# A spectral filter and a channel MLP on one core: the first group's norm written shorter, w1's sums on TensorE, and the folds' rows issued behind other blocks

## The chip, the cores and the metric

The kernel runs on one core of a Trainium2 chip. The metric is the device time of one execution in microseconds. Six actors appear below: PE (TensorE, matmuls and the weight loads before them, PEld), DVE (VectorE), ACT (ScalarE), POOL (GpSimd), SP (SyncE, which here only issues DMAs), and the 16 DMA engines. Every engine works through its own queue in order; an instruction that waits on a semaphore holds up whatever is queued behind it on that engine.

## The reference

x has 2048 rows of 448 numbers. It is normalised over the row, and two branches of the result are added to x:

```
xn = layernorm(x)
A  = irfft2(rfft2(xn) * (w_r + 1j * w_i))
h  = gelu(layernorm(xn) @ w1)                  # 448 x 448
hs = (h with its four column groups shifted by +1, -1, +2, -2 rows) @ w2
x1 = xn + hs
B  = x1 + gelu(layernorm(x1) @ w3) @ w4        # 448 x 1792, 1792 x 448
out = x + A + B
```

All inputs are fp32. The two norms in a row (the second one inside branch B) differ only by the eps terms, so the kernel gets both scales from one mean and one variance.

## The kernel before, in words

**Tiling.** The rows are split so that row a * 16 + b is partition a of block b: 16 blocks of 128 x 448. They form four groups, `GRP` = [14, 15, 0, 1], [2, 3, 4, 5], [6, 7, 8, 9], [10, 11, 12, 13], in which a shift by one or two rows is a shift to a neighbouring block. A group lies in one tile `xt`.

**Number format.** Matmuls run in fp16 on pairs: a matrix is scaled by a power of two and split into a high half and the rest, and three of the four products are summed in PSUM. For each weight matrix the scale comes from the sum of its squares: ACT squares the matrix and sums along the row (`squares`, L246), DVE adds the few columns up and PE adds over the partitions with a matrix of ones (`powers`, L251 and L258), and DVE takes the exponent out of the bits (L261 to L264) and gives the scale s and its inverse r. `split_w` then makes the halves; for the first quarter of w1 on DVE (L273, L275).

**The head.** SP issues the loads: x of group 0 in two halves, w1, x of group 1, w2, x of group 2, two of the four pieces of w3 (`w3raw`), x of group 3, the other two pieces. PE meanwhile runs `WARM` matmuls of zeros (L890). `stats1` takes mean and variance of each block on DVE (L316, L317). `norm1` makes from them a rough inverse square root, by the integer trick on the float's bits: `va` = variance plus eps terms, for the outer and the inner norm (L342, L343), shift and subtract into `vy` (L344, L345), -mean times that into `nma` (L347). Then each block is normalised in place with it, by the engine that `apply` names (L360 on DVE or POOL, L357 on ACT; in group 0 POOL takes the first 128 columns of the block that ACT has, L355). The exact root is made later, on POOL (`refine`, L368 to L376), and goes in with the scales `gsc` and `cs`. The list passed for group 0 is P, V, V, A, and `mid=squares1` puts ACT's squares of w1 between `nma` and the normalisation.

After that PE turns the blocks of group 0, one quarter of the columns at a time (`turn_pe`, L414), into `pta`; ACT and DVE make the halves (`turn_copy`, L424, L425, into `w4x`), and PE multiplies with w1 (`w1_in`, L465). Each further quarter needs its halves of w1: on POOL L281, L283, L286, L289, on ACT L282, L288. Between PE's matmuls of the first group the rows of group 1 are normalised and turned in the same way (second use of L342 to L360 and L414).

**From h to the MLP.** `w1_unit` makes gelu and halves of h (ACT L486, L488, DVE L489) into `hs` or a piece of `x2mem`, and a transposing DMA on SP turns each block of it into `h` (L492). `w2_mm` multiplies with w2 (L510), for block b from the blocks b - 1, b + 1, b - 2, b + 2. Groups 2 and 3 of x are turned by transposing DMAs too (`turn`, L911). `ln2` normalises for the MLP and turns by DMA (L553, its last block leaves the keys "b0", "b4", "b8" and so on). The MLP runs over pairs of blocks G and pairs of 128 columns of the inner 1792, fp = 0 to 6: `front` (L435, into PSUM `pw`, with gelu on ACT, L774, and halves on ACT and DVE, L777, L778) and `back` (L812, into `acc`).

**The spectral branch** is laid between the MLP's matmuls. `do_fold` loads the rows of x again, two blocks at a time, into one of four buffers (L575: three are `xf`, in the place that w2 and h leave; the fourth is `hgm`), ACT normalises them (L579, L580), POOL folds (L584 to L587), ACT and DVE make halves `xh` (L595, L596), and `step1` multiplies (L605, into `ps`).

**What sets the order.** A planner orders each engine's queue on its own model of time. `behind(key)` pins what is issued inside it behind the instructions that left that key, where they stand on the same engine; it adds an order and no wait. `PACE` pins `step1` of the blocks 0 and 1 behind the MLP's `back` of (0, 6), and so on; `FOLD` pins ACT's part of the folds behind the halves of `front`.

Of the kernel before, what the change touches and what calls it, by code (L numbers as in the profile page):

```python
# [26 lines left out]
WARM = 22  # L27
# [3 lines left out]
EPS = 1e-5  # L31
# [91 lines left out]
def body(tc, nc, x, wf, w1, w2, w3, w4, c_g, c_n, c_small, out):  # L123
# [41 lines left out]
    def xb(b):  # L165
        g, i = WHERE[b]
        return xt[g][:, i]
# [80 lines left out]
    def powers(m, n, key, tag="acc", mid=None, pin=None, down=0):  # L248
# [10 lines left out]
        after["p" + key] = (i.ins,)  # L259
        e = pc.tile([128, 3], I32, name=f"pe{key}")  # L260
# [3 lines left out]
        i = V.tensor_scalar(out=e[:, 2:3], in0=e[:, 0:1], scalar1=1, scalar2=(69 + down) << 23, op0=ALU.mult, op1=ALU.add)  # L264
        after["s" + key] = (i.ins,)
        return e.bitcast(F32)[:, 1:2], e.bitcast(F32)[:, 2:3]
# [28 lines left out]

    def rsqrt(r, a, n, key):
# [3 lines left out]
        V.tensor_single_scalar(i, a.bitcast(I32), 1, op=ALU.logical_shift_right)  # L300
        V.tensor_scalar(out=i, in0=i, scalar1=-1, scalar2=0x5F3759DF, op0=ALU.mult, op1=ALU.add)
# [29 lines left out]
    def norm1(g, apply, seen=0, mid=None):  # L331
# [8 lines left out]
        y = yi.bitcast(F32)  # L340
        with behind(0, 3) if g == 2 else contextlib.nullcontext():
            V.tensor_scalar(out=a[:, n:], in0=mv[:, :n, 1], scalar1=1.0 + EPS, scalar2=EPS * EPS, op0=ALU.mult, op1=ALU.add)  # L342
            V.tensor_scalar(out=a[:, 0:n], in0=mv[:, :n, 1], scalar1=EPS, scalar2=None, op0=ALU.add)  # L343
        V.tensor_single_scalar(yi, a.bitcast(I32), 1, op=ALU.logical_shift_right)  # L344
        V.tensor_scalar(out=yi, in0=yi, scalar1=-1, scalar2=0x5F3759DF, op0=ALU.mult, op1=ALU.add)  # L345
        nm = pc.tile([128, n], F32, name=f"nma{b0}")
        i = V.scalar_tensor_tensor(out=nm, in0=mv[:, :n, 0], scalar=-1.0, in1=y[:, n:], op0=ALU.mult, op1=ALU.mult)  # L347
        if mid:
            mid()
        for k, b in enumerate(bs):  # L350
            y_, m_ = y[:, n + k:n + k + 1], nm[:, k:k + 1]
            if apply[k] is A:
                o = 128 if g == 0 else 0
                if o:
                    P.tensor_scalar(out=xb(b)[:, :o], in0=xb(b)[:, :o], scalar1=y_, scalar2=m_, op0=ALU.mult, op1=ALU.add)  # L355
                with behind("sq", g) if ("sq", g) in after else contextlib.nullcontext():
                    i = A.activation(out=xb(b)[:, o:], in_=xb(b)[:, o:], func=AF.Identity, scale=y_, bias=m_)  # L357
# [841 lines left out]
```

## Time and profile before

| | us |
|---|---|
| median of 3 runs (408.83 to 409.05) | 408.83 |
| the profiled execution | 408.91 |
| its span, first to last instruction | 406.4 |

| engine | idle longest before | us in all, times |
|---|---|---|
| POOL | `e` L735, for ACT | 56.5, 14 |
| ACT | `pw` L774, for PE | 42.6, 34 |
| DVE | `hf` L778, for ACT | 36.8, 25 |
| PE | the first warm-up matmul L890, for DVE | 1.2, 1 |

A row of the profile reads: start in us from the span's first instruction, us, engine, source line, operation, what it writes <- what it reads, partitions x elements and type, how many instructions the row merges, and in brackets how long the engine had been idle before and what ended that. SPq is SP's queue: the duration of a DMA row there is the time of its issue, not of the transfer; the time to landing is told apart. In the rows by stretches stand, after the length, busy us and instructions of PE, PEld, DVE, ACT and POOL, then the granted clock of TensorE, the DMA engines' busy share and GB/s. The chain of work that ended last is followed back from the last instruction; its rows are start, us and what.

### The profile page before, as it was taken

The numbers are of one execution on the slowest core, as the hardware profiler recorded it, in microseconds if no ns is written. First come the engines' busy times: TensorE is split into PE (matmuls) and PEld (weight loads), VectorE is DVE, ScalarE is ACT, GpSimd is POOL, SyncE is SP. The second block draws the span as 40 slices with busy tenths as digits, with TensorE's granted clock in tenths as the row PEclk, the third lists the DMA queues.
The fourth block names the chain that finished last, engine by engine and source line by source line (L and its number), as shares of the span: only waits on it lengthen the run. The fifth ranks groups of instructions, "written<-read, shape, count | busy, mean of one in ns | idle before, by whom it ended". The sixth has DMA issues, their size and how long they took to land.

```text
span 406.4 us, 8829 instructions
## 1 busy us (share of the span) xinstructions
PE 401.0 (99%) x3379; PEld 295.9 (73%) x3379; DVE 304.0 (75%) x664; ACT 268.4 (66%) x465; POOL 173.0 (43%) x270
## 2 busy tenths in 40 slices
PE   8999999999999999999999999999999999999996
PEld 3554556666677877776878878877788888888885
DVE  5989998898554757893677777773588879889645
ACT  4699984984738766862587888776856566444332
POOL 3889803011099746599143434431232264211000
PEclk9999999999999999999999999999999999999999
DMA  8999999905910383417064566632000112233201
GB/s 283 379 245 183 175 176 253 272 2 113 242 57 0 96 276 129 115 34 177 15 147 129 144 151 163 157 93 58 2 2 2 47 45 77 86 96 112 89 2 45
DMA packets 57209, 49.46 MB, mean 122 GB/s; under 512 B 41312, under 2 KB 52192, under 8 KB 57168
## 3 DMA queue, kind: packets, MB, share of 16 engines
q1 hardware_dynamic: 57168, 48.91, 46.1%
q8 instruction: 26, 0.43, 0.5%
q14 instruction: 15, 0.12, 0.1%
HBM read 35.06 MB, written 3.67 MB: 95 GB/s over the span
## 4 chain that ended last, share of the span: by engine, by line
PE 83%; DVE 7%; DMA 3%; ACT 3%; issue 1%; POOL 0%; SPq 0%; DVEq 0%; ACTq 0%
PE pw L435 28%; PE acc L812 22%; PE pw L510 8%; PE pw L465 6%; PE pu L708 3%; PE ps L605 3%; PE pp L662 2%; PE px L679 2%; PE cr L827 2%; PE acc L827 2%; DVE xr L560 1%; DMA out<-xr 1%; PE pe L728 1%; PE py L750 1%; DVE hf L778 1%
## 5 line engine op out<-in xcount | busy, mean ns | idle before, releaser
L435 PE MATMUL pw<-x2mem,w3p 128*128 128x256 f16 x1232 | 149.2, 272 | 0.0
L435 PEld LDWEIGHTS <-w3p 128*128 128x128 f16 x1232 | 118.8, 98 | 19.4
L812 PE MATMUL acc<-w4p,hf 128*128 128x448 f16 x508 | 107.6, 352 | 0.0
L812 PEld LDWEIGHTS <-hf 128*128 128x128 f16 x532 | 51.4, 98 | 35.4
L778 DVE SCALAR_TENSOR_TENSOR hf<-pw,h,hf 128x512 f16<-128x512 f32 x56 | 41.8, 747 | 37.0 <-ACT hf L777 36.8
L774 ACT ACTIVATE pw<-pw,pe 128x512 f32<-128x512 f32 x56 | 36.7, 656 | 42.7 <-PE pw L435 42.6
L777 ACT ACTIVATE hf<-pw,h 128x512 f16<-128x512 f32 x56 | 38.3, 684 | 1.3
L510 PE MATMUL pw<-w2p,h 112*128 112x448 f16 x192 | 39.0, 352 | 0.1
L735 POOL TENSOR_TENSOR e<-e 128x226 f32<-128x226 f32 x16 | 11.0, 688 | 64.0 <-ACT e L732 56.5
L465 PE MATMUL pw<-w1p,w4x 128*128 128x448 f16 x176 | 34.8, 352 | 0.5 <-DVE h L968 0.5
L510 PEld LDWEIGHTS <-h 112*128 112x128 f16 x192 | 18.6, 98 | 16.3 <-DMA h<-x2mem 0.9
L689 POOL TENSOR_TENSOR xr<-te 128x450 f32<-128x450 f32 x16 | 15.7, 981 | 34.1 <-DVE te L687 34.1
L465 PEld LDWEIGHTS <-w4x 128*128 128x128 f16 x176 | 17.0, 98 | 16.4 <-ACT w4x L424 0.7
L697 POOL TENSOR_TENSOR zb<-xr,zb 128x450 f16<-128x450 f32 x16 | 16.2, 1011 | 17.1 <-ACT zb L696 17.1
L742 ACT ACTIVATE vh<-e 128x448 f16<-128x448 f32 x16 | 9.2, 575 | 15.6 <-DVE e L740 15.4
L685 DVE SCALAR_TENSOR_TENSOR te<-px,sc,wc 128x450 f32<-128x450 f32 x16 | 11.0, 686 | 10.3 <-ACT te L684 6.7
L684 ACT ACTIVATE te<-px 64x450 f32<-64x450 f32 x32 | 17.3, 539 | 1.7 <-PE px L679 1.2
L720 ACT ACTIVATE U<-y 113x512 f16<-113x512 f16 x32 | 18.0, 620 | 0.1
L732 ACT ACTIVATE e<-pe 128x452 f32<-128x452 f32 x16 | 8.7, 544 | 12.7 <-PE pe L728 10.2
L712 DVE SCALAR_TENSOR_TENSOR y<-pu,y 113x512 f16<-113x512 f32 x16 | 10.9, 687 | 6.9 <-ACT y L711 6.8
L540 POOL TENSOR_SCALAR y<-xt,nm 128x448 f32<-128x448 f32 x6 | 5.9, 991 | 22.8 <-DMA x2mem<-y 12.9
L584 POOL TENSOR_TENSOR xr<-xf 128x452 f32<-128x452 f32 x6 | 6.7, 1123 | 20.6 <-ACT xf L580 10.5
(207 smaller groups left out, 793.1 us busy)
## 6 DMA issues: line engine op xcount, KB each, us to landing
wc<-wf SPq DMA_DIRECT2D x32, 225.0 KB, 3.8
wl<-wf SPq DMA_DIRECT2D x8, 450.0 KB, 3.9
xt<-x SPq DMA_DIRECT2D x3, 896.0 KB, 10.2
w3raw<-w SPq DMA_DIRECT2D x3, 896.0 KB, 14.0
xf<-x SPq DMA_DIRECT2D x6, 448.0 KB, 3.9
xr<-x SPq DMA_DIRECT2D x12, 224.0 KB, 2.5
out<-xr SPq DMA_DIRECT2D x12, 224.0 KB, 2.0
gn<-c_g SPq DMA_DIRECT2D x16, 128.0 KB, 3.1
```

The lines of the kernel that those rows point to most:

```text
L435: m = T.matmul(ps_out, wp[:, wi + t, cols], xT[:, xi + t, tok], start=t == 0 and wi + xi == 0, stop=t == 3 and wi == 4)
L465: m = T.matmul(pm[:, :D], xTs[g][:, xi + t, 128 * i:128 * i + 128], w1p[:, wi + t], start=t == 0 and p == 0, stop=t == 3 and p == 2)
L510: m = T.matmul(w2b[b][:, :D], hT[g][:112, 4 * hi + k, o:o + 128], w2p[:, wi, k], start=k == 2 and hi + wi == 0, stop=k == 3 and hi == 1)
L684: i = A.activation(out=e[64 * h:64 * h + 64], in_=px_[64 - 64 * h:128 - 64 * h, :2 * DF], func=AF.Copy)
L689: P.tensor_tensor(out=z, in0=t[:, 0], in1=t[:, 1], op=ALU.add)
L697: P.tensor_tensor(out=zv[1], in0=z, in1=zv[0], op=ALU.subtract)
L720: A.activation(out=U[b][:113, p].rearrange("p q (c k) -> p q c k", c=NC), in_=Y1[:113, p, :, :, b], func=AF.Copy)
L774: A.activation(out=pm, in_=pm, func=AF.Gelu_apprx_tanh, scale=r3)
L777: i = A.activation(out=h[:, 0], in_=pv_, func=AF.Copy, scale=h3)
L778: j = V.scalar_tensor_tensor(out=h[:, 1], in0=pv_, scalar=h3, in1=h[:, 0], op0=ALU.mult, op1=ALU.subtract)
L812: m = T.matmul(to, h[:, hi, 2 * f + i], w4p[0][:, wi, 2 * fp + f, r], start=fp == s and f == 0 and hi + wi == 0, stop=fp == e and f == 1 a ...
L827: m = T.matmul(to, h[:, hi, slot] if slot < 4 else g[:, hi, slot - 4], w4f[fp][k][wi], start=k in (0, 6) and fp == 0 and hi == 0, stop=hi ...
```

## The change

- `WARM` goes from 22 to 18 matmuls.
- `guess` makes the rough root in one operation, times -0.5 and plus the constant, where a shift and a multiply-add stood (`norm1` and `rsqrt`).
- `norm1` of group 0 makes only the inner norm's row of `va` and `vy` ahead of the normalisation, and the outer one's behind it (`rough(0)`, `guess`, behind the key ("n", 0)). The other groups keep both in front.
- Group 0 is normalised by V, V, P, V for the blocks 14, 15, 0, 1; block 1 in two pieces, columns 0 to 127 and 128 to 447. ACT has no part in it, and the squares of w1 are issued ahead of `norm1`.
- `norm1` returns `y[:, n:]` in place of `nma`, so the single matmul before the last two warm-up matmuls reads that.
- The sum over w1's five columns of squares is made by PE: five matmuls with the ones into one column of PSUM, the constant column and columns 0 to 2 ahead of the first transposes, column 3 behind them. `powers` is split: `factors` gives s at once and r by a call, which is made after the high half of w1's first quarter.
- The loads of the folds' rows are pinned behind key "b4" (the transpose of block 7 in `ln2`) in place of "b8" (of block 11).

```diff
@@ -24,7 +24,7 @@
 CS = {b: 4 * g + i for b, (g, i) in WHERE.items()}
 PASS = ((0, 0), (0, 1), (1, 0))
 SHIFT = [1, -1, 2, -2]
-WARM = 22
+WARM = 18
 ZPRE = 2.0 ** -7
 UPRE = 2.0 ** -3
 VPRE = 2.0 ** -3
@@ -257,13 +257,21 @@
         with behind(*pin) if pin else contextlib.nullcontext():
             i = T.matmul(pm[:, 0:1], ones, t, start=True, stop=True)
         after["p" + key] = (i.ins,)
+        s, r = factors(pm, key, down)
+        return s, r()
+
+    def factors(pm, key, down=0):
         e = pc.tile([128, 3], I32, name=f"pe{key}")
         V.tensor_scalar(out=e[:, 0:1], in0=pm.bitcast(I32)[:, 0:1], scalar1=1, scalar2=0x7F800000,
                         op0=ALU.logical_shift_right, op1=ALU.bitwise_and)
         V.tensor_scalar(out=e[:, 1:2], in0=e[:, 0:1], scalar1=-1, scalar2=(185 - down) << 23, op0=ALU.mult, op1=ALU.add)
-        i = V.tensor_scalar(out=e[:, 2:3], in0=e[:, 0:1], scalar1=1, scalar2=(69 + down) << 23, op0=ALU.mult, op1=ALU.add)
-        after["s" + key] = (i.ins,)
-        return e.bitcast(F32)[:, 1:2], e.bitcast(F32)[:, 2:3]
+
+        def inverse():
+            i = V.tensor_scalar(out=e[:, 2:3], in0=e[:, 0:1], scalar1=1, scalar2=(69 + down) << 23, op0=ALU.mult, op1=ALU.add)
+            after["s" + key] = (i.ins,)
+            return e.bitcast(F32)[:, 2:3]
+
+        return e.bitcast(F32)[:, 1:2], inverse
 
     def absmax(out_, in_):
         V.tensor_reduce(out=out_, in_=in_, axis=AX.X, op=ALU.max, apply_absolute_value=True)
@@ -293,12 +301,14 @@
+    def guess(i, a):
+        V.tensor_scalar(out=i, in0=a.bitcast(I32), scalar1=-0.5, scalar2=0x5F3759DF, op0=ALU.mult, op1=ALU.add)
+
     def rsqrt(r, a, n, key):
...
-        V.tensor_single_scalar(i, a.bitcast(I32), 1, op=ALU.logical_shift_right)
-        V.tensor_scalar(out=i, in0=i, scalar1=-1, scalar2=0x5F3759DF, op0=ALU.mult, op1=ALU.add)
+        guess(i, a)
@@ -328,7 +338,7 @@
             mvs[g] = pc.tile([128, 4, 2], F32, name=f"mva{GRP[g][0]}")
         stats([xb(GRP[g][k]) for k in ks], f"a{GRP[g][ks[0]]}", mvs[g][:, ks[0]:])
 
-    def norm1(g, apply, seen=0, mid=None):
+    def norm1(g, apply, seen=0):
 
         bs = GRP[g]
         n, b0 = len(bs), bs[0]
@@ -338,27 +348,31 @@
         a = pc.tile([128, 2 * n], F32, name=f"va{b0}")
         yi = pc.tile([128, 2 * n], I32, name=f"vy{b0}")
         y = yi.bitcast(F32)
+        nm = pc.tile([128, n], F32, name=f"nma{b0}")
+
+        def rough(k):
+            V.tensor_scalar(out=a[:, n * k:n * k + n], in0=mv[:, :n, 1], scalar1=1.0 + EPS * k, scalar2=EPS ** (1 + k),
+                            op0=ALU.mult, op1=ALU.add)
+
         with behind(0, 3) if g == 2 else contextlib.nullcontext():
-            V.tensor_scalar(out=a[:, n:], in0=mv[:, :n, 1], scalar1=1.0 + EPS, scalar2=EPS * EPS, op0=ALU.mult, op1=ALU.add)
-            V.tensor_scalar(out=a[:, 0:n], in0=mv[:, :n, 1], scalar1=EPS, scalar2=None, op0=ALU.add)
-        V.tensor_single_scalar(yi, a.bitcast(I32), 1, op=ALU.logical_shift_right)
-        V.tensor_scalar(out=yi, in0=yi, scalar1=-1, scalar2=0x5F3759DF, op0=ALU.mult, op1=ALU.add)
-        nm = pc.tile([128, n], F32, name=f"nma{b0}")
-        i = V.scalar_tensor_tensor(out=nm, in0=mv[:, :n, 0], scalar=-1.0, in1=y[:, n:], op0=ALU.mult, op1=ALU.mult)
-        if mid:
-            mid()
+            rough(1)
+            if g:
+                rough(0)
+        guess(yi[:, 0 if g else n:], a[:, 0 if g else n:])
+        V.scalar_tensor_tensor(out=nm, in0=mv[:, :n, 0], scalar=-1.0, in1=y[:, n:], op0=ALU.mult, op1=ALU.mult)
         for k, b in enumerate(bs):
-            y_, m_ = y[:, n + k:n + k + 1], nm[:, k:k + 1]
+            x_, y_, m_ = xb(b), y[:, n + k:n + k + 1], nm[:, k:k + 1]
             if apply[k] is A:
-                o = 128 if g == 0 else 0
-                if o:
-                    P.tensor_scalar(out=xb(b)[:, :o], in0=xb(b)[:, :o], scalar1=y_, scalar2=m_, op0=ALU.mult, op1=ALU.add)
-                with behind("sq", g) if ("sq", g) in after else contextlib.nullcontext():
-                    i = A.activation(out=xb(b)[:, o:], in_=xb(b)[:, o:], func=AF.Identity, scale=y_, bias=m_)
+                i = A.activation(out=x_, in_=x_, func=AF.Identity, scale=y_, bias=m_)
                 after["na", g] = (i.ins,)
             else:
-                i = apply[k].tensor_scalar(out=xb(b), in0=xb(b), scalar1=y_, scalar2=m_, op0=ALU.mult, op1=ALU.add)
+                for c in ((slice(0, 128), slice(128, D)) if not g and k == 3 else (slice(0, D),)):
+                    i = apply[k].tensor_scalar(out=x_[:, c], in0=x_[:, c], scalar1=y_, scalar2=m_, op0=ALU.mult, op1=ALU.add)
                 after["n" if apply[k] is V else "np", g] = (i.ins,)
+        if not g:
+            with behind("n", 0):
+                rough(0)
+                guess(yi[:, 0:n], a[:, 0:n])
 
         q, z = (pc.tile([128, 2 * n], F32, tag=f"v{t}", bufs=2, name=f"v{t}{b0}") for t in "qz")
         w, r = (pc.tile([128, 2 * n], F32, name=f"v{t}{b0}") for t in "wr")
@@ -391,7 +405,7 @@
             P.tensor_scalar(out=nm1, in0=nm1, scalar1=-1.0, scalar2=None, op0=ALU.mult)
             for k, b in enumerate(bs):
                 xn_scale[b], xn_bias[b] = r1st[:, k:k + 1], nm1[:, k:k + 1]
-        return refine, gain, scales, nm
+        return refine, gain, scales, y[:, n:]
 
     after = {}
 
@@ -571,7 +585,7 @@
     def do_fold(b0):
         f = xf_buf[b0 // 2 % 4]
         X = f.rearrange("p b s d -> p (b s d)")[:, 0:2 * D + 2].rearrange("p (b d) -> p b d", b=2)
-        with behind("b8"):
+        with behind("b4"):
             after["X", b0] = (SY.dma_start(X[:, :, 0:D], xv[:, b0:b0 + 2]).ins,)
         with behind("f", *FOLD[b0 // 2]):
             for i in range(2):
@@ -934,11 +948,9 @@
         w4f[fp] = [[x[:, i] for i in range(2)] for x in (b[0][0], b[1][0], b[1][1], t4)]
         w4f[fp] += [t1] + [[x[:, i] for i in range(2)] for x in (t2, t3)]
 
-    def squares1():
-        for t in range(4):
-            n = 128 if t < 3 else 64
-            i = squares(m1[:n, t:t + 1], w1s[:n, t])
-        after["sq", 0] = (i.ins,)
+    for t in range(4):
+        n = 128 if t < 3 else 64
+        squares(m1[:n, t:t + 1], w1s[:n, t])
 
     def warm_on(src, n):
 
@@ -946,11 +958,22 @@
         with behind("on"):
             warm_up(n)
 
-    n1 = [norm1(0, [P, V, V, A], mid=squares1)]
+    n1 = [norm1(0, [V, V, P, V])]
     warm_on(n1[0][3], 2)
-    pts = [turn_pe(0, 0)]
-    with behind("n", 0), behind("T", 0):
-        s1, r1 = powers(m1, 4, "1", "mm")
+    pm = bank("mm", "pm1")
+
+    def norm_of(ks):
+        for k in ks:
+            i = T.matmul(pm[:, 0:1], ones, m1[:, k:k + 1], start=k == 4, stop=k == 3)
+        after["p1"] = (i.ins,)
+
+    norm_of([4, 0, 1, 2])
+    with behind("p1"):
+        pts = [turn_pe(0, 0)]
+    with behind("T", 0):
+        norm_of([3])
+    with behind("n", 0):
+        s1, r1 = factors(pm, "1")
     with behind("p1"):
         pts.append(turn_pe(0, 1))
     h_alloc(0)
@@ -964,6 +987,8 @@
             turn_copy(0, t, pts[t])
         with behind("a0", t):
             after["w1", t] = split_w(w1p[:, t], w1p[:, 4 + t], w1s[:, t], s1, P if t > 1 else xr[:, 0:D]) if t else (hi, low())
+    with behind("w1", -1):
+        r1 = r1()
     h1 = pc.tile([128, 1], F32, name="h1")
     V.tensor_scalar(out=h1, in0=s1, scalar1=2.0 ** -5, scalar2=None, op0=ALU.mult)
     for t in range(3):
```

## The prediction

> **What bounds the kernel now.** I read the page's busy shares first, then the busy time by stretches, then the idle time of PE.
>
> ```profile
> PE 401.0 (99%) x3379; PEld 295.9 (73%) x3379; DVE 304.0 (75%) x664; ACT 268.4 (66%) x465; POOL 173.0 (43%) x270
> ```
>
> ```profile
> 9.00:400.00 391.00, 390.05 (x3328) 290.46 (x3329) 296.74 (x635) 264.32 (x456) 170.07 (x257) 1.00 0.46 119
> ```
>
> ```profile
> PE pw L465 <- DVE h L968: 0.5, 1, 0.5
> ```
>
> TensorE is busy for 390.05 of the 391 us between 9 and 400. The longest wait in that stretch is 0.5 us, just before the first real matmul. So the time is a fixed amount of matmul work plus whatever precedes it, and an edit on another engine gains only what it lets PE begin earlier and then keep. The profiled execution took 408.91 us for a span of 406.4; 2.51 us lie around the span. The median of the runs is 0.08 lower.
>
> The head of the kernel is the first place that the change touches. The timeline by instruction, cut to the chain:
>
> ```profile
> 1.22 7.16 PE L890 MATMUL wps<-x2mem 128*128 128x512 f16 x22 [1.22 <-DVE x2mem L188]
> ...
> 5.84 2.04 PEld L890 LDWEIGHTS <-x2mem 128*128 128x128 f16 x10 [0.23 <-issue]
> ...
> 7.14 0.17 DVE L342 TENSOR_SCALAR va<-mva 128x4 f32<-128x4 f32 x1
> 7.22 0.16 DVE L343 TENSOR_SCALAR va<-mva 128x4 f32<-128x4 f32 x1
> 7.41 0.17 DVE L344 TENSOR_SCALAR vy<-va 128x8 int32<-128x8 int32 x1
> 7.62 0.17 DVE L345 TENSOR_SCALAR vy<-vy 128x8 int32<-128x8 int32 x1
> 7.82 0.16 DVE L347 SCALAR_TENSOR_TENSOR nma<-mva,vy 128x4 f32<-128x4 f32 x1
> 8.02 1.26 DVE L360 TENSOR_SCALAR xt<-xt,vy,nma 128x448 f32<-128x448 f32 x2
> 8.22 0.28 PE L945 MATMUL wps<-nma,ones 128*128 128x4 f32 x2
> 8.36 0.59 PE L890 MATMUL wps<-x2mem 128*128 128x512 f16 x2
> 8.90 0.19 ACT L246 ACTIVATION_READ_ACCUMULATOR xr<-w1s 64x1 f32 x1
> 9.00 0.64 ACT L357 ACTIVATE xt<-xt,nma,vy 128x320 f32<-128x320 f32 x1
> 9.03 0.57 POOL L355 TENSOR_SCALAR xt<-xt,vy,nma 128x128 f32<-128x128 f32 x1
> 9.82 0.28 PE L258 MATMUL pm<-pt,ones 128*128 128x1 f32 x2
> 10.14 0.16 DVE L261 TENSOR_SCALAR pe<-pm 128x1 int32<-128x1 int32 x1 [0.79 <-PE pm L258]
> 10.52 0.45 DVE L273 TENSOR_SCALAR w1p<-w1s,pe 128x448 f16<-128x448 f32 x1
> 11.12 0.92 PE L465 MATMUL pw<-w1p,w4x 128*128 128x448 f16 x4 [0.52 <-DVE h L968]
> ```
>
> Small operations that depend on each other start about 0.20 us apart (7.41, 7.62, 7.82, 8.02); two that do not, 0.08 (7.14, 7.22). Block 1 is normalised last, by POOL to 9.60 and ACT to 9.64. Its transpose and then the sum over w1 (9.82) follow, the power of two at 10.14, the first half of w1 at 10.52, and the first real matmul at 11.12.
>
> The second place is where this work next meets something that does not come from it. First the chain that ended last, then the SP queue with the loads and the transposes of h, then the load of w3 by its tile, then busy time by stretches (the two columns before the end are the granted clock and the DMA share, the last GB/s):
>
> ```profile
> 30.34 3.40 DMA h<-x2mem
> 33.78 4.23 PE pw L510 x21
> ```
>
> ```profile
> 8.27 0.33 SPq L217 DMA_DIRECT2D w3raw<-w  x1
> ...
> 25.00 2.50 SPq L492 DMA_TRANSPOSE h<-hs  x1
> 27.62 2.62 SPq L492 DMA_TRANSPOSE h<-hs  x2
> 30.34 2.64 SPq L492 DMA_TRANSPOSE h<-x2mem  x2
> ```
>
> ```profile
> DMA to landing us min/median/max: 11.8/15.8/19.2
> ```
>
> ```profile
> 10.00:24.00 14.00, 13.48 (x84) 8.25 (x84) 12.97 (x40) 9.28 (x16) 12.15 (x30) 1.00 1.01 387
> 24.00:28.00 4.00, 4.00 (x22) 2.07 (x22) 3.39 (x9) 4.00 (x9) 3.92 (x6) 1.00 0.98 125
> ```
>
> The reader is to see an anchor. PE takes up w2 at 30.70 (row below) and at 33.78 goes on with the transposed h of block 1, which SP issued at 30.34 and which landed at 33.74. SP issues these transposes back to back, one per 1.3 us or so, except the first: it starts at 25.00 and holds the queue for 2.50 us, to 27.50. The slowest load of w3, issued at 8.27, lands 19.2 us later, at 27.47. The DMA engines have been full up to there (share 1.01, then 0.98). So I read the first transpose as held by the tail of the weight loads. The end of that tail is bytes over bandwidth, and nothing in the first group's chain moves it.
>
> ```profile
> 30.70 7.31 PE L510 MATMUL pw<-w2p,h 112*128 112x448 f16 x36
> 33.78 0.11 PEld L510 LDWEIGHTS <-h 112*128 112x128 f16 x2 [0.52 <-DMA h<-x2mem]
> ```
>
> Of the 36 matmuls 21 follow the wait, so 15 precede it. One takes 0.19 us (7.31 for 36, less the wait), 15 take 2.85, and PE was through with them at about 33.53. It idles 0.25 us there already.
>
> **The change part by part.**
>
> 1. The scale of group 0. Two steps go from DVE's chain: the second row of `va` (0.08) and the shift (0.20), so `nma` comes 0.28 earlier, at 7.54, and the normalisation starts at 7.74.
> 2. Who normalises. ACT's 0.64 and POOL's 0.57 for block 1 go; POOL takes block 0, and VectorE takes 14, 15 and 1 in two pieces. The pair on VectorE took 1.26, so it is done at 9.00. The trace has no 128-column piece on VectorE. It lies between the 0.17 of a 4-column operation and the 0.45 of a 448-column one (L273); I take 0.20, nearer the small one since fixed cost shows there, and 0.35 for the other 320 columns. Block 1 is whole at 9.55, its first columns at 9.20. The last transpose of the first quarter follows at 9.27 where it now comes at about 9.66, after POOL's 9.60.
> 3. w1's sums. The reduction on DVE goes. PE adds five columns itself: four matmuls ahead of the transposes, one behind. One fp32 matmul of this kind, in two passes, took 0.14 from its start to the next instruction (8.22 to 8.36), and 0.28 by its own row. Four are 0.56 to 1.12, start after the two warm-up matmuls (8.3), wait for ACT's third square until about 8.4, and end between 8.9 and 9.5. The normalisation of block 15 on VectorE, to 9.00, covers all of that but the last 0.5, and block 1's, to 9.20, another 0.2: I take no cost, with 0.25 kept for the range. The fifth needs the last square, read out at 9.09, and falls behind the transposes at about 9.43. From there to the first matmul on w1 it took 1.30 (9.82 to 11.12): 10.73. I add 0.05 for `rough(0)` and `guess`, which DVE may run just before the power of two, and have 10.78, **0.34 earlier**, with bounds of 0.10 and 0.45.
> 4. Warm-up. Ten weight loads in 2.04 us are 0.216 us per matmul, so four fewer end 0.86 earlier, at about 7.4. The matmul that follows waits for `vy`, at about 7.5, and PE idles 0.1 to 0.4 us that it idled elsewhere before. Cost 0, if the clock stays up (below).
> 5. The other groups and `rsqrt` lose one small operation each (0.20 at most), beside a PE that is full.
> 6. Downstream of the head. The anchor takes the 0.34 back: PE reaches the wait at 33.19 instead of 33.53, h still lands at 33.74, and the idle time grows from 0.25 to 0.59. **Sum to the end: 0.00**, bounds -0.59 (the anchor moves freely) and +0.25.
> 7. The folds' x. The four DMAs of the first round leave the place behind block 11's transpose for one behind block 7's. Rows of SP, ACT, DVE and PE:
>
> ```profile
> 104.94 2.01 SPq L575 DMA_DIRECT2D xf<-x  x3
> ```
>
> ```profile
> 109.32 1.41 ACT L579 ACTIVATE xf<-xf,nm,vw 128x448 f32<-128x448 f32 x2 [2.19 <-DMA xf<-x]
> 115.79 1.79 DVE L596 TENSOR_TENSOR xh<-xf,xh 128x452 f16<-128x452 f32 x2 [2.76 <-ACT xh L595]
> ```
>
> ```profile
> 90.62 2.44 PE L510 MATMUL pw<-w2p,h 112*128 112x448 f16 x12
> ...
> 115.95 1.68 PE L812 MATMUL acc<-w4p,hf 128*128 128x448 f16 x8
> 117.47 1.50 PE L605 MATMUL ps<-csm,xh 128*128 128x128 f16 x24
> ```
>
> The buffers are free once the last w2 matmul is through, at 93.06, so the loads need not wait for them. Issued some 5 us earlier they take away ACT's wait of 2.19. That chain ends in `xh` at 117.58, just when PE comes to `ps` at 117.47. But `step1` is pinned behind the last product of the MLP's first two blocks, and that product runs right up to 117.47. So PE cannot take `ps` sooner, and it did not wait for it: gain 0, with 2.2 us of slack in place of none. That slack is needed only if PE comes earlier here. The price is 2.7 us of SP (2.01 for three, and a fourth) ahead of the transposes of blocks 8 to 11. Those are read by the MLP of blocks 8 to 11, after that of blocks 0 to 7, so 0 again. If that cover were gone, PE would wait 2.7 us at most.
>
> The sum is the profiled execution's own 408.91 less 0.00. Against the median that is **408.8**.
>
> **The rivals.**
>
> A, the forecast: the anchor holds. For it: a queue that is held until 27.50 beside a load that lands at 27.47, and 0.25 us of idle time at 33.78. Its own range is 408.4 to 409.2, from 0.4 either way for a newly drawn order of the queues. 408.8, chance 0.38.
>
> B: the transposes of h follow the head, since the first one was slow for a reason of its own. For it: the row shows a duration and not a cause. Then PE keeps 0.34, and at the most the 0.25 of idle time too, so 0.34 to 0.59, and I take 0.47: 408.4, chance 0.18.
>
> C: the planner, which draws the order anew from the earlier times, also puts ready work in front of the late h. Then the head gains its upper bound of 0.45, the 0.25 goes, and the 0.5 us before the first matmul shrinks by some 0.3 on top: 1.0 us, 407.8. Against it: SP's queue stands back to back there, and what follows on PE hangs on that queue too. Chance 0.21, as it stands for every way of gaining more than the head.
>
> D, on the other side: PE's clock falls back. The 22 warm-up matmuls took 7.00 us (1.22 to 8.22), and at 0.216 each they would take 4.75, so a cold stretch costs 2.25. [...] Less the 0.34 and the 0.25 that is 1.66: 410.5, chance 0.08. [...]
>
> [...]
>
> E, also slower: group 1 is turned later. PE's next transposes stood with no room behind POOL:
>
> ```profile
> 15.60 1.03 POOL L289 TENSOR_TENSOR w1p<-w1s,w1p 128x448 f16<-128x448 f32 x1
> 18.51 0.95 POOL L360 TENSOR_SCALAR xt<-xt,vy,nma 128x448 f32<-128x448 f32 x1
> 19.56 1.05 PE L414 MATMUL pta<-ident,xt 128*128 128x128 f32 x8
> ```
>
> POOL ends block 2 at 19.46, and PE takes it at 19.56. POOL is busy for 12.15 of the 14 us from 10 to 24, DVE for 12.97. If the new order puts one more piece like L289 ahead of L360, PE stands 1.03 later, and with two 2.06; 0.34 and 0.25 are covered. That leaves 0.44 to 1.47, the middle 0.95: 409.8, chance 0.15. It decides from 0.6 us of delay on. For it: DVE has two normalising pieces more; against it: POOL has one fewer.
>
> **How the numbers follow.** 0.2% is 0.8 us, about what a measurement of this kernel can tell from no change. C alone is faster by more than that: 0.21. A and B stay within it: 0.56. D and E are slower: 0.23. The predicted time is A's. The range reaches from just below C to just above E, 407.7 to 410.0, and leaves out D and the far ends of the others.
>
> **What would show it.** Right: `nma` near 7.55, the first matmul on w1 near 10.8, the first transpose of h issued near 24.6 yet held to 27.5, PE's wait at 33.78 grown to about 0.6, `xf` issued before 100 and no wait of ACT for it, `ps` still near 117.5. Wrong: the second transpose issued well ahead of 27.6 (B, C), matmuls of 448 columns at twice 0.19 us after 10.8 (D), PE idle near 19.5 (E), or a stall of PE past 100 that the trace of before does not have.

## The result, and the profile after

The changed kernel took 408.12 us (median of 16 runs, 407.40 to 408.39), the kernel before 408.93 (16 runs, 408.34 to 410.03) in the same rounds: a ratio of 0.9975, 95% interval [0.9968, 0.9983]. In later rounds it was 408.03 against 408.89, 0.9978 [0.9967, 0.9988]. So it is faster by 0.81 to 0.86 us, just over the 0.8 us that the prediction took as the line. The range held the time; "no change" was the wrong side of that line.

Where the 0.85 us are is best seen by splitting each run's time in its span, from the first instruction to the last, and what lies around the span, the rest of the execution's time. The medians of the later rounds:

| | time | span | around the span |
|---|---|---|---|
| before (35 runs) | 408.89 | 406.5 | 2.38 |
| after (12 runs) | 408.03 | 406.25 | 1.80 |
| difference | -0.86 | -0.25 | -0.58 |

Two thirds of the gain lie outside the span, a place that the prediction carried over as a constant. The profiled execution of the changed kernel took 407.72 for a span of 405.9.

The page's busy shares after (busy time, share, instructions):

```profile
PE 400.4 (99%) x3383; PEld 296.7 (73%) x3383; DVE 304.2 (75%) x657; ACT 267.5 (66%) x464; POOL 170.1 (42%) x269
```

The head, from the timeline of DVE and of PE (start, duration, then the instructions):

```profile
7.34 0.17 DVE L354 TENSOR_SCALAR va<-mva 128x4 f32<-128x4 f32 x1
7.54 0.17 DVE L305 TENSOR_SCALAR vy<-va 128x4 int32<-128x4 int32 x1
7.75 0.16 DVE L362 SCALAR_TENSOR_TENSOR nma<-mva,vy 128x4 f32<-128x4 f32 x1
7.95 1.87 DVE L370 TENSOR_SCALAR xt<-xt,vy,nma 128x448 f32<-128x448 f32 x4
...
10.38 0.45 DVE L281 TENSOR_SCALAR w1p<-w1s,pe 128x448 f16<-128x448 f32 x1
```

```profile
7.07 0.50 PE L967 MATMUL pm<-m,ones 128*128 128x1 f32 x4
...
9.68 0.28 PE L967 MATMUL pm<-m,ones 128*128 128x1 f32 x2
9.82 0.63 PE L428 MATMUL pta<-ident,xt 128*128 128x128 f32 x4
10.98 0.92 PE L479 MATMUL pw<-w1p,w4x 128*128 128x448 f16 x4 [0.52 <-DVE pe L270]
```

From `va` to the first real matmul it took 3.98 us before (7.14 to 11.12) and 3.64 after (7.34 to 10.98). That is 0.34 shorter, the number of the prediction. On the clock only 0.14 shows, because `va` itself began 0.20 later in this execution: DVE got x's first half 0.20 later (it began on it at 4.68 in place of 4.48, after a wait for the load) and had no wait from there to `va`.

The 0.34 is the best that this head does, not what it always does. In the second profile of the same changed kernel the stretch took 3.85 (6.97 to 10.82). ACT, then PE:

```profile
8.00 0.58 ACT L246 ACTIVATE xr<-w1s 128x448 f16<-128x448 f32 x1 [0.29 <-DMA w1s<-w]
```

```profile
8.72 0.38 PE L967 MATMUL pm<-m,ones 128*128 128x1 f32 x2
8.96 0.63 PE L428 MATMUL pta<-ident,xt 128*128 128x128 f32 x4
```

ACT's third square waits for its load of w1, PE's sum over that column for the square, and the transposes stand behind the sum. Over the seven profiles that have this head unaltered, those of the experiments below included, the stretch took 3.64 to 4.02, median 3.76; over the five with the old head 3.98 to 4.11, median 3.98. So the new head is some 0.2 shorter by the medians.

SP's transposes of h and PE at w2:

```profile
24.85 4.76 SPq L506 DMA_TRANSPOSE h<-hs  x3
29.72 2.63 SPq L506 DMA_TRANSPOSE h<-x2mem  x2
```

```profile
30.55 6.97 PE L524 MATMUL pw<-w2p,h 112*128 112x448 f16 x36
```

The 36 matmuls took 6.97 in place of 7.31: the wait for h, 0.34, is gone in this profile, where the prediction had it grow to 0.6. The h of block 1 landed at 33.00 in place of 33.74.

The folds' x (SP, then ACT, then PE):

```profile
98.32 1.56 SPq L589 DMA_DIRECT2D xf<-x  x3
```

```profile
106.61 1.40 ACT L593 ACTIVATE xf<-xf,nm,vw 128x448 f32<-128x448 f32 x2
```

```profile
115.47 1.68 PE L826 MATMUL acc<-w4p,hf 128*128 128x448 f16 x8
116.98 1.50 PE L619 MATMUL ps<-csm,xh 128*128 128x128 f16 x24
```

They are issued 6.6 us earlier, ACT has no wait for them, and `ps` follows the product without a gap.

And the end. The DMA view of the stretch from 406.8 to 412, that is, behind the last instruction, of the kernel before and then of the changed one (a queue's line gives packets, MB, share of 16 engines):

```profile
q14 instruction: 1, 0.01, 0.6%
```

```profile
DMA packets 0, 0.00 MB, mean 0 GB/s; under 512 B 0, under 2 KB 0, under 8 KB 0
```

Before, one packet of 8 KB on an instruction queue moves at 408.61, 2.2 us behind the end of the span. After, there is none.

### The profile page after: what moved, and what is told of

Its sections match the earlier page's. It is cut to its first block, busy times and chain, and to the rows that moved or that the text cites. A ratio compares the mean times of both kernels' runs of the same rounds, so it can differ in the third digit from the quotient of the medians.

```text
span 405.9 us, 8826 instructions
## 1 busy us (share of the span) xinstructions
PE 400.4 (99%) x3383; PEld 296.7 (73%) x3383; DVE 304.2 (75%) x657; ACT 267.5 (66%) x464; POOL 170.1 (42%) x269
## 4 chain that ended last, share of the span: by engine, by line
PE 86%; DVE 8%; DMA 3%; ACT 1%; issue 1%; SPq 0%; DVEq 0%
PE pw L449 28%; PE acc L826 22%; PE pw L524 9%; PE pw L479 8%; PE pu L722 3%; PE ps L619 3%; PE pp L676 2%; PE px L693 2%; PE cr L841 2%; PE acc L841 2%; DVE xr L574 1%; DMA out<-xr 1%; PE pe L742 1%; PE py L764 1%; DVE hf L792 1%
## 5 line engine op out<-in xcount | busy, mean ns | idle before, releaser
L757 DVE TENSOR_TENSOR vh<-e,vh 128x448 f16<-128x448 f32 x16 | 10.0, 622 | 7.1 <-ACT vh L756 7.1
L683 ACT ACTIVATE pf<-pp 64x450 f16<-64x450 f32 x16 | 8.7, 541 | 9.7 <-PE pp L676 7.8
```

## The experiments

**How much one profile says: the kernel before, again**

> The kernel before, unchanged, for its spans. Theory T: of the 0.8 to 1.0 us between the two kernels about 0.7 lies outside the span, because DVE's stream of instructions is 7 longer before and one more block of instructions is fetched behind the end of the program (in the profile an 8 KB packet of kind instruction 2.2 us after the span, which the changed kernel lacks). T expects 2.5 us outside the span in every run, against 1.75 to 1.85 in the runs of the changed kernel, and spans with a median only 0.1 to 0.5 above the changed kernel's 406.3. Rival R: the gain is made inside the span by the shorter head; R expects spans about 0.8 above 406.3 and the same 1.8 us outside in most runs.

408.79, ratio 0.9995 [0.9986, 1.0004]; span 406.5, around it 2.39. So T has the place of the gain: the span is only 0.2 above the 406.3 of the changed kernel's first runs, and R's 0.8 is out. T's 2.5 "in every run" did not come: the eleven runs have 1.99 to 2.51. The profile of this run differs from the first one's in just the places on which the prediction was built (PE at w2, PE's weight loads at `ps`, ACT at the folds' x):

```profile
30.57 6.97 PE L510 MATMUL pw<-w2p,h 112*128 112x448 f16 x36
...
118.09 0.56 PEld L605 LDWEIGHTS <-xh 128*128 128x128 f16 x10 [0.28 <-DVE xh L596]
...
109.79 1.41 ACT L579 ACTIVATE xf<-xf,nm,vw 128x448 f32<-128x448 f32 x2 [3.12 <-DMA xf<-x]
```

Here PE does not wait at w2, and it does wait at `ps`, by 0.33 (24 matmuls took 1.83 in place of 1.50). In the first profile it was the other way round. Call a place where PE may have to wait a gate: in these two profiles the same kernel loses about a third of a microsecond, once at the one gate and once at the other.

**The pin alone, on the old order**

```
-        with behind("b8"):
+        with behind("b4"):
```

> The kernel before with nothing but the folds' pin moved from block 11 to block 7; on the engines only the order of SP's queue differs. Both runs of the kernel before that have a profile lose some 0.35 us of PE once: either at 33.8 behind the transposed h (first profile, 0.36, and then no wait at ps) or at 117.0 behind xh (second profile, 0.34, and then none at 33.8). Theory 'second gate': the late xf loads fix the time at which xh is there (117.6 to 118.0), so that whatever PE gains earlier is lost at ps; with the loads issued near 99, xh ends near 115 and the gate is gone. Then the span falls by 0.1 to 0.35 against the kernel before, I say 0.2, to about 406.4, the time outside the span stays at 2.4 (VectorE's stream has its old length), and the ratio is 0.9993. Rival 'the pin is worth nothing' (step 7): span within 0.1 of 406.65. Rival 'price of the queue': the transposes of blocks 8 to 11 land 2.7 us later and PE waits for them: span longer by 0.5 or more.

408.14, ratio 0.9986 [0.9975, 0.9998]. The span fell from 406.5 to 406.0, more than the 0.2 that was said (by 0.5, interval 0.0 to 0.9, by drawing the runs anew; a second batch, below, makes it firmer); around it 2.12 and not the 2.4 that was said. SP, ACT and PE in its profile:

```profile
97.68 1.55 SPq L575 DMA_DIRECT2D xf<-x  x3
...
106.74 1.40 ACT L579 ACTIVATE xf<-xf,nm,vw 128x448 f32<-128x448 f32 x2
...
30.73 6.99 PE L510 MATMUL pw<-w2p,h 112*128 112x448 f16 x36
...
117.18 1.50 PE L605 MATMUL ps<-csm,xh 128*128 128x128 f16 x24
```

Neither gate costs anything to speak of here (6.99 and 1.50). "The pin is worth nothing" falls, and so does "the price of the queue": the last transpose of blocks 8 to 11 ends 2.1 us later (106.92 for 104.84) and nobody waits.

**All of the change but the pin**

```
-        with behind("b4"):
+        with behind("b8"):
```
(on the changed kernel)

> The changed kernel with the folds' rows pinned behind block 11 again (key b8); only SP's order differs. The prediction's step 7 expects no change: 408.1, ACT's wait of 2.2 us before the first fold back, no idle time of PE. The rival, that the pin carries part of the gain, expects PE to wait before ps or later and 0.2 to 0.5 us more.

409.40, ratio 1.0009 [1.0000, 1.0017]: not faster than before in spite of 1.80 around the span, since the span is 407.6, 1.3 over the changed kernel and 1.1 over the kernel before. Both expectations miss: step 7's of no change, and the rival's of 0.2 to 0.5. SP, ACT, PE:

```profile
107.52 1.56 SPq L589 DMA_DIRECT2D xf<-x  x3
...
111.71 1.41 ACT L593 ACTIVATE xf<-xf,nm,vw 128x448 f32<-128x448 f32 x2 [4.25 <-DMA xf<-x]
...
118.20 0.28 PE L619 MATMUL ps<-csm,xh 128*128 128x128 f16 x2 [0.51 <-ACT xh L609]
119.06 0.84 PE L619 MATMUL ps<-csm,xh 128*128 128x128 f16 x12 [0.58 <-DVE xh L610]
```

The late pin costs more in the new order than in the old, because the transposes ahead of the loads have become later. ACT's timeline shows why, first of the kernel before, then of this one:

```profile
100.03 0.64 ACT L774 ACTIVATE pw<-pw,pe 128x512 f32<-128x512 f32 x1
100.62 1.23 ACT L548 ACTIVATE y<-y,vs 128x448 f16<-128x448 f32 x2
101.76 0.67 ACT L777 ACTIVATE hf<-pw,h 128x512 f16<-128x512 f32 x1
102.33 1.03 ACT L291 ACTIVATE w4p<-x2mem,pe 128x896 f16<-128x896 f32 x1
```

```profile
100.03 0.64 ACT L788 ACTIVATE pw<-pw,pe 128x512 f32<-128x512 f32 x1
...
101.28 0.67 ACT L791 ACTIVATE hf<-pw,h 128x512 f16<-128x512 f32 x1
101.85 1.03 ACT L299 ACTIVATE w4p<-x2mem,pe 128x896 f16<-128x896 f32 x1
102.78 1.22 ACT L562 ACTIVATE y<-y,vs 128x448 f16<-128x448 f32 x2
```

The last two casts of `y` now stand behind a product of the gelu and a cast of w4, 2.16 us later. The last two transposes start at 104.85 and 106.18 (102.20 and 103.53 before), and with the pin behind them `xf` follows at 107.52.

**Which part of the change reorders ACT: step 5 alone on the kernel before**

```
-        V.tensor_single_scalar(i, a.bitcast(I32), 1, op=ALU.logical_shift_right)
-        V.tensor_scalar(out=i, in0=i, scalar1=-1, scalar2=0x5F3759DF, op0=ALU.mult, op1=ALU.add)
+        V.tensor_scalar(out=i, in0=a.bitcast(I32), scalar1=-0.5, scalar2=0x5F3759DF, op0=ALU.mult, op1=ALU.add)
```
(in `rsqrt`, and the same in `norm1`)

> The kernel before with step 5 alone: the guess of the inverse square root in one operation of VectorE everywhere (group 0's chain is 0.20 shorter by it); who normalises, w1's sums, the warm-up and the pin stay. The planner's order of ACT with this edit has the last two casts of y for blocks 10 and 11 behind a gelu, a product of it and a cast of w4, as in the changed kernel. Theory 'the new order makes the late pin dear': the last two transposes start near 104.9 and 106.2, xf is issued near 107.5, ACT waits some 4 us, PE waits 1 to 1.7 at ps; span 407.3 to 407.7, outside 1.9 (819 instructions on VectorE), ratio 1.001. Rival 'what was lost with the late pin came from the rebuilt head': span 406.4 or less, as its head is 0.2 shorter, ratio 0.998.

409.23, ratio 1.0014 [1.0005, 1.0023]; span 407.4 as the first theory expected, around it 1.79 where 1.9 was said. SP and PE:

```profile
106.97 1.56 SPq L573 DMA_DIRECT2D xf<-x  x3
...
117.72 0.29 PE L603 MATMUL ps<-csm,xh 128*128 128x128 f16 x2 [0.32 <-ACT xh L593]
118.58 1.52 PE L603 MATMUL ps<-csm,xh 128*128 128x128 f16 x19 [0.58 <-DVE xh L594]
```

One small operation fewer on VectorE each time a root is guessed, and the planner draws an order that costs 0.9 us of span with the late pin. The rebuilt head is not needed for that loss.

**The anchor: the head made later, and w3 out of the way**

```
         rough(1)
         ...
+        for _ in range(0 if g else 3):
+            V.tensor_scalar(out=a[:, n:], in0=a[:, n:], scalar1=1.0, scalar2=None, op0=ALU.mult)
         guess(yi[:, 0 if g else n:], a[:, 0 if g else n:])
```

> The changed kernel with three more multiplications by 1 of the four variances, each dependent on the one before, ahead of the guess of group 0: 0.20 each, so the first real matmul comes 0.6 later; the order of PE, ACT, POOL and SP is otherwise the same (one of the matmuls for w1's sums moves up). Theory 'the transposes of h follow the head' (rival B): h of block 1 lands 0.6 later too (33.6 in place of 33.0 in the profile), the wait at w2 is as before, and the span grows by 0.5 to 0.6, to 406.85. Theory 'anchor' (step 6): h lands where it did, PE's wait there shrinks by up to what it was (0.0 to 0.3 in the profiles of the changed kernel), and the span grows by 0.3 or less, to at most 406.6. Outside the span: VectorE's stream is 823; 1.8 if its end does not reach the bound, 2.4 to 2.7 if it does.

408.63; span 406.5, around it 2.13. Against all 28 runs of the changed kernel itself the median of the spans is 0.2 longer, with a 95% interval of -0.1 to 0.5 (by drawing the runs anew), so by these the full 0.6 of "follow" is out; against the six runs of the kernel with six idle memsets (405.9, below), it is 0.6 [0.2, 0.9]. PE and SP:

```profile
11.55 0.92 PE L481 MATMUL pw<-w1p,w4x 128*128 128x448 f16 x4 [0.52 <-DVE pe L270]
...
25.42 4.67 SPq L508 DMA_TRANSPOSE h<-hs  x3
30.20 2.65 SPq L508 DMA_TRANSPOSE h<-x2mem  x2
```

Compare the changed kernel's second profile (SP):

```profile
24.69 5.19 SPq L506 DMA_TRANSPOSE h<-hs  x3
29.99 2.65 SPq L506 DMA_TRANSPOSE h<-x2mem  x2
```

The first transpose starts 0.73 apart, the fourth 0.21; h of block 1 landed at 33.52 and 33.32. Beside the changed kernel's first profile, where the transposes went through best (24.85 and 29.72, landed at 33.00), it follows almost in full. So neither theory has it whole. The queue takes up part of a change of the head, how much of it these runs do not settle (the span grew by 0.2 or by 0.6 for a head 0.6 later), and it is not a rigid stop.

```
-    load_w3([2, 3])
 ...
+    with behind("h", 0, 3):
+        load_w3([2, 3])
```

> The changed kernel with the last two of w3's four loads issued behind the last transpose of h of group 0 instead of ahead; the planner then orders PE, DVE and ACT anew from about 40 us on, so the total is read with care. Theory 'anchor': the first transpose of h then takes 1.3 as the others do (it took 1.36 to 2.5, the second 1.3 to 1.9), the four lie 1.33 apart from 24.9, the last lands near 32.0, and PE has no wait at w2; span 0 to 0.3 shorter for that. Rival 'a reason of their own': the first two still take 1.6 or more on average and the last lands at 33.0 or later.

414.57, ratio 1.0136 [1.0115, 1.0156], so as a version it is bad; its SP queue answers the question:

```profile
24.80 4.27 SPq L505 DMA_TRANSPOSE h<-hs  x3
29.17 1.34 SPq L505 DMA_TRANSPOSE h<-x2mem  x1
30.56 0.58 SPq L217 DMA_DIRECT2D w3raw<-w  x1
31.20 0.48 SPq L219 DMA_DIRECT2D w3raw<-w  x1
31.79 1.60 SPq L505 DMA_TRANSPOSE h<-x2mem  x1
33.49 4.66 SPq L505 DMA_TRANSPOSE h<-hs  x1
```

With w3's last two loads out of the way three transposes take 4.27 in place of 4.67 to 5.19 in the rows above (4.57 to 5.39 over the thirteen other profiles), and h of block 1 lands at 32.38, earlier than in any other profile. So it is w3's tail that holds them, by the one profile of this kernel. The same loads, now ahead of the fifth and sixth transpose, hold those: the sixth takes 4.66, the fifth lands at 39.41, and PE's 36 matmuls at w2 take 13.62 in place of 6.97. That is where the 6 us go, which the expectation of a span 0 to 0.3 shorter did not see.

**Is the head worth anything once the rest is done?** The kernel before, with the pin moved and with the eight memsets of the small sums on POOL instead of VectorE, beside the changed kernel in the same rounds:

```
-        V.memset(m, 0.0)
-        V.memset(m[:, n:], 2.0 ** -65)
+        P.memset(m, 0.0)
+        P.memset(m[:, n:], 2.0 ** -65)
 ...
-        with behind("b8"):
+        with behind("b4"):
```

> The kernel before with two edits and nothing of the head: the folds' pin moved to block 7 (span 406.0 in place of 406.5 by itself) and the eight memsets of the small sums moved from VectorE to POOL (1.92 outside the span in place of 2.42 by itself). Theory 'the pin and the end of the program are all': the two add up, span 406.0, outside 1.9, time 407.9 to 408.0, ratio 0.998, no slower than the changed kernel beside it. Rival 'the head gives its 0.3 as well': this kernel stays 0.3 above the changed kernel, near 408.3.

> The changed kernel itself, so that it stands in the same rounds as the others. From its first runs: span 406.3, outside 1.80, time 408.1, ratio 0.998. If its span is nearer to the 405.9 of the same kernel with six idle memsets, the two batches differ by 0.4 and differences of that size between batches say nothing.

408.34, ratio 0.9989 [0.9979, 0.9998] (span 406.25, around it 2.08), against 408.03 (406.25, 1.80) for the changed kernel again, as in its first runs (406.3, 1.80). The first theory has the time 0.4 too low and the rival has the right time for a wrong reason: it put the 0.3 inside the span, where the two are equal; the difference lies around it, 2.08 where 1.9 was said. Taken together, the 24 runs with the old head and the early pin have a span 0.4 shorter [0.2, 0.6] than the 92 of the kernel before beside them, the 28 of the changed kernel 0.3 shorter [0.1, 0.6]. So the pin accounts for all that the span shows, and the new head, some 0.2 shorter, for nothing that these runs can tell. One case was not run: the order that step 5 brings, with the early pin and the old head. So it is not shown that the head is worth nothing; a small gain of the head could be taken back by a small loss through that order. No version tried beats the changed kernel by more than the runs' scatter; the one with six idle memsets, 407.80, has too few runs to say so.

**What lies around the span**

Counted in the trace, VectorE has 826 instructions in the kernel before, waits included, and 820 in the changed one. In twelve of the fourteen profiles a packet on the instruction queue q14 moves when that count is 701 to 704; in the two with eight and with fourteen idle memsets (below) it comes at 691. With fourteen, another moves when the count is 831, 140 further. In the changed kernel's first profile five of the fifteen packets within the span move at counts of 191, 318, 447, 576 and 704, in steps of 127 to 129. The theory: the packet at the end is VectorE's next one, and moves when its count comes near 832, one such step past 704. ACT has 563 instructions and POOL 349 in the changed kernel and in those with idle memsets alike, so what differs between these isn't theirs. Four kernels change that count. The kernel before with only the memsets moved to POOL (the first half of the diff above):

> The kernel before with 8 small memsets of the head moved from DVE to POOL, which is idle there; the order of PE, ACT and SP is the same. T expects 1.8 us outside the span and no fetch behind the end, 0.7 below the kernel before (408.2), with its span unchanged. R expects no change against the kernel before (408.9).

408.62, ratio 0.9989 [0.9980, 0.9998]; span 406.7 as the kernel before in those rounds (406.7), around it 1.92 in place of 2.42, and no packet. That is T's way, with a gain of 0.4 to 0.5 where it said 0.7. By the trace the count is 819, one more than eight moved instructions give.

The changed kernel with idle memsets ahead of everything on VectorE:

```
+    pad = pc.tile([128, 8], F32, name="pad")
+    for i in range(8):
+        V.memset(pad[:, i:i + 1], 0.0)
```

> The changed kernel with 8 memsets of one column each put at DVE's start, where DVE waits for x until 4.5 us. T expects DVE's stream to cross the block's bound again: 2.5 us outside the span, a fetch behind the end, the span unchanged (406.3), 408.8 in all, about the time before. R expects 408.1, as the changed kernel.

408.38, ratio 0.9983 [0.9974, 0.9991]; span 406.4, around it 1.99: neither the 2.5 of T nor the 1.8 of R. A packet moved, 1.8 us behind the end.

With six of them (826, the count of before):

> The changed kernel with six one-column memsets ahead of everything on VectorE, in its idle time: VectorE's stream then has 826 instructions as in the kernel before, and the order of all other engines is that of the changed kernel. Theory 'fetch behind the end': a block of VectorE's instructions is fetched once its count passes 832, and with 826 that falls after the last instruction of the program, as in the kernel before: outside the span 2.4 (as there), span 406.3 as in the changed kernel, time 408.7. With 828 it was 1.99 and with 820 it was 1.80. Rival 'outside the span belongs to the changed kernel': 1.8, time 408.1.

407.80 (6 runs), ratio 0.9968 [0.9956, 0.9980]; around the span 1.88 and no packet: a miss. Perhaps 826 is the edge: the kernel before itself has 1.96 to 2.04 around its span, not 2.25 to 2.56, in 11 of 92 runs. Whether the packet is missing in those is not shown, as none of them was profiled.

With fourteen (834):

> The changed kernel with fourteen idle one-column memsets at the start of VectorE: 834 instructions, past 832. Theory 'fetch behind the end': the 8 KB packet now falls at or before the last instructions, some 0.5 us or less behind the end of the span or inside it, and costs nothing: outside 1.8 to 1.9. Rival 'more instructions on VectorE, more time outside': 2.1 or more. Span as in the changed kernel.

409.43, ratio 1.0013 [1.0005, 1.0022]. Around the span 1.81, as said, but the span itself is 407.6, so the packet does not cost nothing. The packet came at 405.12, into the last store. Up to the stores the execution ran as in the changed kernel's second profile: PE's last matmuls start at 401.81 in both. The DMA view of that store, first here, then of the changed kernel (KB each, us from issue to landing):

```profile
q14 instruction: 1, 0.01, 0.6%
issues: line engine op xcount, KB each, median us to landing
out<-x2mem SPq DMA_DIRECT2D x1, 112.0 KB, 3.0
```

```profile
out<-x2mem SPq DMA_DIRECT2D x2, 112.0 KB, 1.8
```

So the packet follows VectorE's count, if not to the instruction, and what goes with it depends on where it falls:

| kernel | VectorE's count | packet | around the span |
|---|---|---|---|
| before | 826 | 2.2 behind the end | 2.38 to 2.47 |
| pin alone | 827 | 1.8 behind | 2.12 |
| 8 memsets | 828 | 1.8 behind | 1.99 |
| 14 memsets | 834 | in the last store | 1.81, span +1.3 |
| memsets on POOL | 819 | none | 1.92 |
| after, after with the late pin, step 5 alone | 820, 819, 817 | none | 1.80, 1.80, 1.79 |
| 6 memsets | 826 | none | 1.88 |
| memsets on POOL, pin | 820 | none | 2.08 |
| later head | 823 | none | 2.13 |

Eight memsets taken from VectorE took the packet from the kernel before, and 0.50 from what lies around its span (2.42 to 1.92). The same eight taken from the kernel with the early pin took its packet too, but only 0.04 (2.12 to 2.08). So some 0.4 of the 0.58 between the two kernels goes with a packet 2.2 us behind the end, and one 1.8 us behind goes with little; that the packet is the cause is inferred from the two coming and going together. The rest is a base, 1.79 to 2.13 in the kernels without a packet, that differs by kernel and stays within 0.11 over the runs of one; what sets it stays open.

## Why the prediction was right and wrong

The range held, and in part by luck. The sum had nothing for the span, where the pin brought some 0.3 to 0.4, and nothing for what lies around it, where 0.58 went; the range was wide for other reasons, the ends of C and E.

**Steps 1 and 2** were right. `nma` came 0.41 after `va` in place of 0.68, 0.27 shorter for 0.28. DVE's four normalising pieces took 1.87 where 1.81 was worked out: the two estimates of 0.20 and 0.35 were 0.33 and 0.43, but their starts lay only 0.06 later in sum.

**Step 3** came out to the number in the first profile: from `nma` to the first real matmul 3.23 (7.75 to 10.98), worked out 3.24. The planner set three of the four early sums ahead of the last two warm-up matmuls, from 7.07 on. But over the seven profiles it was 3.23 to 3.61. The step had the early sums at no cost; in the second profile the third square, which waited for w1's load, made them cost 0.2. The step's own bounds for the gain, 0.10 to 0.45, hold the 0.2 of the medians better than its 0.34.

**Step 4** was right about the clock, and D is out: behind the 3.7 us from 7.24 (the last long warm-up matmul) to 10.98, with two warm-up matmuls in them, the four matmuls took 0.92, as before and as in all fourteen profiles. The slow pace that D's 2.25 us comes from stands at the start of both profiles (the warm-up's weight loads 0.43 us apart to 5.46 before and to 5.04 after, then about 0.22); that PE falls back to it later is shown by no run. The cost of 0 was not always right. The 18 warm-up matmuls ended at 7.24 in the first profile, near the 7.4 that was worked out, but between 6.58 and 8.16 over the profiles with this head; where they ended at 8.16 (six idle memsets) PE came late to the sums and the stretch from `va` took 4.02, no less than before.

**Step 5** failed: "one small operation each (0.20 at most), beside a PE that is full" has no cost in itself, but the planner drew another order from it. That order costs 0.9 us of span with the late pin; with the early pin the changed kernel, which has it, stands level with the old order.

**Step 6** was right in its sum, and in its mechanism in part. w3's tail does hold the transposes (the first three take 4.27 without it, 4.57 to 5.39 with it), and what the head gains is not seen behind them: PE was through with its 36 matmuls at w2 at 37.54 to 38.22 in the five profiles with the old head (median 37.72) and at 37.52 to 37.94 in six with the new one (median 37.64). But the anchor is not rigid, as the later head shows. The prediction took h's landing at 33.74 as a fixed point; over the thirteen profiles in which the loads stand as they did it was 32.77 to 34.03, wider than the head's whole gain, and 33.74 and 33.15 for the kernel before alone. Its main evidence, a queue held to 27.50 beside a load that lands at 27.47, was a coincidence of one profile: the load of w3 that landed last there was another, the fourth, at 28.21, and in the changed kernel's first profile the first transpose was through at 26.21, ahead of both (27.25 and 28.40), and the second was held instead, to 28.26. PE's wait at 33.78 did not grow to 0.6 in the changed kernel, where it was 0 and 0.17; with fourteen idle memsets, where the first real matmul came earliest (10.71), it was 0.52. B's "second transpose issued well ahead of 27.6" did come true (26.41), but it did so in the kernel before as well (26.43 in its second profile), so it was no sign of B.

**Step 7** is the step that failed by its size. That PE "did not wait for it: gain 0" was true of the one profile. Its own next sentence, that the slack is "needed only if PE comes earlier here", was the answer: in the second profile of the same kernel PE came earlier and waited 0.33. The pin on the old order shortened the span by 0.4 [0.2, 0.6] over its two batches, and in the order that step 5 brings it is worth 1.3. In the first profile the last `xh` was there at 117.58 and PE had come to `ps` at 117.47; in the second it was 118.04 and 117.00, and PE, which needs that piece only after the first 14 matmuls, had to wait. A few tenths decide whether this gate costs anything.

**The time around the span** was the larger miss: "2.51 us lie around the span" was carried over as a constant. It fell by 0.58, and in the balance of the parts this is most of the result. That VectorE loses instructions could be read from the diff, and the packet behind the end was in the trace of before.

The rivals: D and E did not come (PE stood nowhere near 19.5). B's 408.4 and C's 407.8 lie nearer to the time (408.12, then 408.03) than A's 408.8, but neither mechanism made it: the gain is not the head's, as B has it, and of C there is no ready work in front of a late h, and the 0.52 ahead of the first matmul is still there.

## What to carry over

A second unchanged profile of the same kernel costs little, and a gate whose slack is a few tenths of a microsecond in one profile is to be booked as a gate in some of the runs, not as free; a gain that is read off one profile is likewise one draw. Split the time in its span and what lies around it before pricing a change to either, and look what the trace still does behind the last instruction. Where a planner orders the work, an operation less on an engine that is not the bottleneck can move casts two microseconds elsewhere, so a load should be pinned to what it needs and not to a place in a queue that the planner moves.

## What was not expected of the hardware

Instructions come in while the kernel runs, on q14 in packets of 8 KB, fifteen of them within the span before and after. Two of them could be put down to VectorE by its count: one at 701 to 704 (691 in two profiles) and, where there is one, another at 826 to 831. In the kernel before, where a packet comes 2.2 us behind the last instruction, the time around the span was 0.4 to 0.5 us longer than without one; 1.8 us behind, it was 0.04 longer in the one pair of kernels that tells. Where one fell beside the last store, that store took 3.0 us from issue to landing in place of 1.8, and the span was 1.3 us longer. Eight or fourteen one-column memsets in an engine's idle time thus changed the kernel's time by 0.1 and by 0.3% without touching its work.
